# Two load queues for the chunk halves and a double-buffered conversion of w_out pieces in a one-core retention + MoE kernel

## The chip, the core and the metric

The kernel runs on one core of a Trainium2 chip. The metric is the device time of one execution in microseconds (us); the number compared is the median of several runs. Engine names are those of the profile: PE is TensorE (PEld its weight loads), DVE is VectorE, ACT is ScalarE, POOL is GpSimd, SP is SyncE, which here only issues DMAs. "SPq" and "ACTq" are the instruction queues of SP and ACT.

## What is computed

The reference chains three parts:

```
scores = q k^T / 8, times gamma_h^(i-j) for j <= i, else 0        (8 batches, 8 heads, 576 x 64)
x      = (scores v) gathered to 4608 tokens x 512
x      = gelu_sigmoid(x w_in) w_out                                (512 -> 2048 -> 512)
logits = x phi                                                     (4608 x 32)
d      = softmax of logits over the 4608 tokens;  slots = d^T x    (32 slots x 512)
slot results = relu(slots w1[e]) w2[e]                             (8 experts, 4 slots each)
out    = softmax of logits over the 32 slots, times slot results   (4608 x 512)
```

w_in and w_out come as 64-bit floating point numbers and are turned to 32-bit on the chip.

## The kernel before, in words

**Attention part.** The tokens are cut into 72 chunks of 64. For a chunk `g`, `scores(g)` (L182) multiplies queries and keys on PE, GpSimd scales the keys (L191) and VectorE masks the scores (L193, L194). `chunk_out(g)` (L196) makes the chunk's output on PE (L201, L202; it needs the masked scores), VectorE scales it into `xs` (L208, two buffers), ScalarE rounds it (L209) and GpSimd makes the remainder (L210). `state(g)` (L212) carries the running state. Each chunk's data lie in one of four `pack` buffers, which `load_chunk` (L173) fills with two half loads of 256 KB each, one for partitions 0 to 63 (L175) and one for partitions 64 to 127 (L176), both issued by SP. Parts of the packs that no load writes are cleared once by VectorE (L163, L164).

**Main part.** 384 tokens (6 chunks) make a block; there are 12. For each of 16 feature slices `fc`, `main_fc` (L331) does 12 matmuls into a `hp` buffer (three of them exist, L335 and L339) and ScalarE applies the gelu (L341). `turn_fc` (L343) turns the result: VectorE transposes it (L362), and after slices 7 and 15 SP issues 16 DMAs in a row that move it to the buffer `nat` (L368). `logits_group`, `softmax_part` and `slots_part` follow for the same or the block before. The chunks of block n+1 are worked in block n, at the slices in `CHUNK_AT`.

**Weights.** `load_raw` (L262) brings w_in (kind I) and a transposed w_out (kind O) in 32 loads of 512 KB into staging places: six early ones, then four rows of `ring` and `raw_tile` (L256). `convert` (L275) turns 64-bit numbers to 32-bit with one ScalarE (L279) and two VectorE instructions (L280, L281). The list `START` (L49) writes out the order of all this for block 0: T a chunk load, C constants, P phi, L the next raw load, A the next chunk step, I and O a conversion, M a slice of block 0.

**Pieces of w_out.** The slots need w_out once more in its natural layout. In blocks 1 to 8, four pieces per block (32 in all) are loaded (L318, 256 KB, at `fc % 4 == 0`), converted and stored to DRAM (L323, 128 KB, at `fc % 4 == 2`). All use the single buffer `raw`: load, conversion and store share it, so the load of a piece can start only when the store before it has landed.

**Expert weights.** `prefetch` (L449) brings 72 loads of 512 KB into places that come free late in the kernel: one `raw`, `NW2` = 9 in `pw2` after the attention buffers are closed, and others; the last blocks and the tail consume them.

**Who sets the order.** The source gives a program order. A planner (L745) then fixes, at build time and by its own estimate of times, one order for each engine and queue; it may take an instruction ahead of its place when its inputs and buffers are free in that estimate. On the chip each engine and queue goes strictly through its own list: what waits holds up everything behind it.

Of the kernel before, what the change touches and what calls it, by code (L numbers as in the profile page):

```python
# [9 lines left out]
F32 = mybir.dt.float32  # L10
F32R = mybir.dt.float32r
I32 = mybir.dt.int32
# [14 lines left out]
C = 64  # L27
NPB = S // C
NP = H // 2
# [4 lines left out]
NFC = DFF // 128  # L34
# [1 line left out]
NTILE = NT // 128  # L36
GF = 4
HF = NFC // 2
NW2 = 9
NW3, NW4 = 6, 5  # L40
DH = DM // 2

# [1 line left out]
PC = NP * C  # L44
# [2 lines left out]


START = (  # L49
    "T0 C T1 L L T2 L P A L A L L I L A L I L A L A I L A A I L M O L I L M O L I L A M O L I L M O I A M O I M A O I "  # L50
    "L M O I L A M I L O L L L L M A O I L M O I L M A O I L M I L O L L L M O M O M O M O"
).split()

ORDER = "IIIIOIOIOIOIOIOIOIIOOIOIOIIOOOOO"
EARLY = 18

# [56 lines left out]
def tile_kernel(ctx, tc, qkv, w_in, wo_t, w_out, phi, w1, w2, consts, out):  # L115
    nc = tc.nc
    pe, act, dve, pool, sp = nc.tensor, nc.scalar, nc.vector, nc.gpsimd, nc.sync
# [5 lines left out]
    px = ctx.enter_context(tc.tile_pool(name="px", bufs=1, reuse_waits="tile"))  # L123
# [4 lines left out]
    pa = att_ctx.enter_context(tc.tile_pool(name="pa", bufs=2, side="right", reuse_waits="tile"))  # L128

    ring = px.tile([128, 4, 2, 512], F32, name="ring")  # L130
# [27 lines left out]
    Q1, V0, KTB, KN, KTA, Q0, V1 = range(7)  # L158
    early_raw = pm.tile([128, 6, 1024], F32, tag="nat", name="early_raw")
    packs = []  # L160
    for i in range(NPACK):
        t = pa.tile([128, 7, NP, C], F32, name=f"pack{i}", bufs=1)
        dve.memset(t[0:C, 0:KN], 0.0)  # L163
        dve.memset(t[C:128, KTA:7], 0.0)  # L164
        packs.append(t)
    kts = []
    for i in range(2):
        t = pa.tile([128, 2, NP, D], F32, name=f"kt{i}", bufs=1)
# [4 lines left out]
    def load_chunk(g):  # L173
        t = packs[g % NPACK].rearrange("p c a d -> p (c a d)")
        sp.dma_start(t[0:C, KN * PC:7 * PC], qkv[g, 0:C])  # L175
        sp.dma_start(t[C:128, 0:KTA * PC], qkv[g, C:128])  # L176

    how = {"sub": {}}
    St = {}
# [16 lines left out]
    def chunk_out(g):  # L196
        n, off = divmod(g * C, NB)
        t = packs[g % NPACK]
        Op = ps.tile([128, NP, C], F32, tag="r", name="Op", bufs=3)
        for p in range(NP):  # L200
            pe.matmul(Op[0:C, p, :], t[:, V0, p], t[:, Q0, p], start=True, stop=True)  # L201
            pe.matmul(Op[C:128, p, :], t[:, V1, p], t[:, Q1, p], start=True, stop=True)  # L202
        if n not in xh:
            x = (pg if n % 2 == LAST % 2 else pb).tile([128, 2, NDC, NB], F32R, tag="x", name="x", bufs=1)
            xh[n], xl[n] = x[:, 0], x[:, 1]
        cols_ = slice(off, off + C)
        xs = pa.tile([128, NP, C], F32, tag="xs", name="xs")
        dve.tensor_tensor(xs, Op, osc, op=ALU.mult)  # L208
        act.copy(xh[n][:, :, cols_], xs)  # L209
        pool.tensor_tensor(xl[n][:, :, cols_], xs, xh[n][:, :, cols_], op=ALU.subtract)  # L210
# [31 lines left out]
    def chunk_items(n):  # L242

        if n >= NBLK:
            return []
        chunk_at = CHUNK_AT_LAST if n == LAST else CHUNK_AT
        return [(chunk_at[i], lambda g=g: chunk(g)) for i, g in enumerate(range(n * NB // C, (n + 1) * NB // C))]
# [4 lines left out]

    wo_dram = pd.tile([NFC // 2, 128, 2, DM], F32, name="wo_dram")
    wt, raws = {}, {}
    raw_tile = px.tile([128, 1024], F32, tag="raw", name="raw", bufs=1)
    late = [ring[:, i].rearrange("p a f -> p (a f)") for i in range(4)] + [raw_tile]  # L256

    free = {True: [early_raw[:, i] for i in range(6)], False: late}
    order = list(ORDER)
    loaded = {"I": 0, "O": 0}  # L260

    def load_raw():  # L262
        kind = order.pop(0)
        i = loaded[kind]
        loaded[kind] += 1
        early = sum(loaded.values()) <= EARLY and len(free[True]) > 0
        t = free[early].pop(0)
        raws[kind, i] = t, early
        (act if kind == "I" and i < 3 else sp).dma_start(
            t.bitcast(I32), (w_in if kind == "I" else wo_t)[i].bitcast(I32))  # L270

    def give_back(place):
# [2 lines left out]
    def convert(raw, out):  # L275
        two = raw.bitcast(I32).rearrange("p (f w) -> p f w", w=2)
        upper, lower = two[:, :, 1], two[:, :, 0]
        out = lower if out is None else out
        act.activation(upper.bitcast(F32), upper.bitcast(F32), AF.Prelu, scale=2.0 ** -112, alpha=2.0 ** 32)  # L279
        dve.tensor_scalar(lower, lower, 29, None, op0=ALU.logical_shift_right)  # L280
        dve.scalar_tensor_tensor(out, upper, 3, lower, op0=ALU.logical_shift_left, op1=ALU.bitwise_or)  # L281
        return upper.bitcast(F32), out.bitcast(F32)
# [28 lines left out]
            give_back(raws.pop(("O", 4 * g + a)))  # L311


    raw_n = {}

    def load_natural(i):
        raw_n[i] = px.tile([128, 1024], F32, tag="raw", name="raw", bufs=1)
        sp.dma_start(raw_n[i][:, 0:512].bitcast(I32), w_out[i // 2].bitcast(I32)[:, i % 2 * 512:i % 2 * 512 + 512])  # L318

    def convert_natural(i):  # L320
        t = raw_n.pop(i)
        _, w = convert(t[:, 0:512], t[:, 512:768].bitcast(I32))
        sp.dma_start(wo_dram[i // 4, :, i // 2 % 2, i % 2 * 256:i % 2 * 256 + 256], w)  # L323


    ring_pre = ring.rearrange("p a b f -> p (a b f)")[:, 0:4 * NB * 2].rearrange(
# [44 lines left out]
    def logits_group(n, g):  # L371
        if g == 0:
            Lg[n] = ps.tile([128, NB], F32, tag="L", name="Lg")
        for fl in range(GF):
            pe.matmul(Lg[n][32 * fl:32 * fl + 32, :], Wp[:, g * GF + fl, :], gT[n, g][:, fl, :],  # L375
                      start=(g == 0), stop=(g == NFC // GF - 1))
# [69 lines left out]
    def place_in(pool_, tag, bufs):  # L446
        return lambda: pool_.tile([128, 1024], F32, tag=tag, name="wx", bufs=bufs)

    def prefetch(place=None):  # L449
        if not todo:  # L450
            return
        key = todo.pop(0)
        if place is None:
            place = places.pop(0)
        t = place()
        places.append(place)
        if key[0] == 0:
            src = wo_dram[key[1]]
        elif key[0] == 1:
            src = w1[key[1], key[2] * 128:(key[2] + 1) * 128, :].rearrange("(c p) d -> p c d", p=128)  # L460
        else:
            _, c, e, i = key
            src = w2[c, e, i]
        t = t.rearrange("p (c d) -> p c d", c=src.shape[1])
        sp.dma_start(t, src)
        wx[key] = t

    def prefetch_views(t):
        for i in range(t.shape[1]):
            prefetch(lambda i=i: t[:, i])  # L470
# [40 lines left out]
    for n in range(1, NBLK):  # L511
        items = chunk_items(n + 1)
        ni, done = len(items), 0
        for fc in range(NFC):
            main_fc(n, fc)
            if n < LAST:
                turn_fc(n, fc)
            if fc % 4 == LOGITS_AT and fc >= 4:
                logits_group(n, (fc - 4) // 4)
            if fc == SOFTMAX_AT:  # L520
                logits_group(n - 1, 3)
                softmax_part(n - 1)
                if n == LAST:
                    combine_part(0, NTILE - NT128)
            if fc == SLOTS_AT:
                slots_part(n - 1)
            if 1 <= n <= NFC // 2:
                i = 4 * (n - 1) + fc // 4
                if fc % 4 == 0:
                    load_natural(i)  # L530
                elif fc % 4 == 2:
                    convert_natural(i)
            while done < ni and items[done][0] <= fc:
                items[done][1]()
                done += 1
            if n == LAST - 1:
                if fc == 9:
                    prefetch_views(pb.tile([128, 3, 1024], F32, tag="pre", name="wx", bufs=1))
                if done == ni and pw2 is None:
                    att_ctx.close()  # L540
                    prefetch(place_in(px, "raw", 1))
                    pw2 = ctx.enter_context(tc.tile_pool(name="pw2", bufs=NW2, side="right", reuse_waits="tile"))
                    for _ in range(NW2):
                        prefetch(place_in(pw2, "w", NW2))
            if n == LAST:
                if fc == 0:
                    prefetch_views(pb.tile([128, 3, 1024], F32, tag="x", name="wx", bufs=1))
                prefetch(place_in(pw, "w", NFC))
                if fc == 4:
                    prefetch_views(ring.rearrange("p a b f -> p a (b f)"))  # L550
                for i in range(5 if fc == 4 else fc > 4):
                    turn_fc(n, fc - (4 - i if fc == 4 else 0))
# [197 lines left out]
```

## Time and profile before

| | us |
|---|---|
| runs shown | 814.96, 816.33, 812.89 (median 814.96) |
| the profiled execution's own time | 817.49 |
| its span in the profile | 815.5 |
| PE busy in the span | 734.8 (90%) |
| DVE, ACT, POOL busy | 394.0, 241.2, 165.7 |

"Busy" is the time in which an engine had an instruction in work. The 12 blocks, the start (block 0 with the weight conversion) and the tail (experts and output) have different limits, so they are read one by one. PEclk is the granted clock of TensorE as a share of full speed (1.00 is 2.4 GHz, 0.50 is 1.2 GHz).

### The profile page before, as it was taken

What the parts mean: (1) busy time and instruction counts of PE and PEld (TensorE: products, weight loads), DVE (VectorE), ACT (ScalarE), POOL (GpSimd) and SP (SyncE); (2) the same over time, 40 slices, a digit from 0 to 9 for tenths busy, and PEclk for the clock granted to TensorE, in tenths of its full rate; (3) what the DMA queues carried; (4) which work ended last, traced back from release to release, by engine and by line L of the source; (5) the groups of instructions that cost most, each with busy time, mean ns of one, the idle gap of its engine ahead of it and who ended that gap; (6) DMA issues with size and microseconds to landing.
All of it is one profiled execution on the core that took longest, in us unless ns stands there. A gap on an engine that the chain in (4) does not pass through costs nothing.

```text
span 815.5 us, 17707 instructions
## 1 busy us (share of the span) xinstructions
PE 734.8 (90%) x7056; PEld 594.1 (73%) x7056; DVE 394.0 (48%) x1172; ACT 241.2 (30%) x491; POOL 165.7 (20%) x241
## 2 busy tenths in 40 slices
PE   3479979989989999799899799999999999996994
PEld 2468858768778697686787688887888878782453
DVE  5966373545356446536435555464455542313223
ACT  2433342323123213113123223231232312431323
POOL 4663230112121122111211212222112110000000
PEclk9679989999989999999999999999999999998997
DMA  9993772376476566565565666654547538898988
GB/s 247 330 228 100 192 236 74 108 164 160 121 165 156 124 149 151 123 155 137 123 159 127 150 151 145 152 130 95 136 108 157 130 64 315 270 374 315 409 345 334
DMA packets 76977, 148.98 MB, mean 183 GB/s; under 512 B 11232, under 2 KB 47840, under 8 KB 76896
## 3 DMA queue, kind: packets, MB, share of 16 engines
q1 hardware_dynamic: 76464, 146.29, 64.2%
q10 hardware_dynamic: 432, 1.57, 0.6%
q8 instruction: 55, 0.90, 0.5%
q14 instruction: 26, 0.21, 0.1%
HBM read 101.16 MB, written 13.63 MB: 141 GB/s over the span
## 4 chain that ended last, share of the span: by engine, by line
PE 49%; DMA 26%; SPq 12%; DVE 6%; issue 3%; ACT 2%; POOL 0%; ACTq 0%; DVEq 0%
PE hp L339 28%; DMA wo_dram<-raw 12%; SPq L368 9%; DMA raw<-in_moe_w_out_dram 9%; DMA early_raw<-in_moe_w_in_dram 4%; PE Lg L375 3%; PE Sg L423 2%; PE Op L201 2%; PE so_ps L670 2%; PE h_ps L606 2%; PE Sp L188 2%; SPq L176 1%; SPq L175 1%; PE St L227 1%; ACT raw L279 1%
## 5 line engine op out<-in xcount | busy, mean ns | idle before, releaser
L339 PE MATMUL hp<-x,w 128*128 128x384 f32 x2304 | 448.0, 348 | 9.7 <-ACT gT L341 5.8
L339 PEld LDWEIGHTS hp<-x,w 128*128 128x128 f32 x2304 | 404.1, 192 | 42.2 <-issue 18.4
L341 ACT ACTIVATE gT<-hp 128x384 f32<-128x384 f32 x192 | 91.1, 488 | 173.2 <-PE hp L339 170.5
L191 POOL TENSOR_TENSOR kt<-pack,cs 64x256 f32<-64x256 f32 x128 | 80.4, 628 | 254.8 <-PE St L228 78.1
L210 POOL TENSOR_TENSOR x<-xs,x 128x256 fp32r<-128x256 f32 x72 | 55.7, 773 | 224.2 <-ACT x L209 206.0
L362 DVE STREAM_TRANSPOSE ring<-gT 128x128 f32<-128x128 f32 x240 | 54.4, 280 | 79.6 <-ACT gT L341 79.4
L201 PEld LDWEIGHTS Op<-pack 128*64 128x64 f32 x576 | 43.4, 145 | 53.1 <-DVE pack L193 33.0
L201 PE MATMUL Op<-pack 128*64 128x64 f32 x576 | 56.0, 238 | 27.4 <-DVE pack L193 27.4
L362 DVE STREAM_TRANSPOSE pre<-gT 128x128 f32<-128x128 f32 x264 | 59.0, 278 | 44.8 <-ACT gT L341 44.8
L280 DVE TENSOR_SCALAR raw<-raw 128x256 int32<-128x256 int32 (+1 forms) x36 | 11.8, 327 | 124.8 <-DMA raw<-in_moe_w_out_dram 114.5
L187 PE MATMUL Sp<-pack 128*64 128x64 f32 x576 | 52.5, 238 | 14.7 <-DMA pack<-in_qkv_dram 14.7
L279 ACT ACTIVATE raw<-raw 128x256 f32<-128x256 f32 (+1 forms) x36 | 16.9, 471 | 161.8 <-DMA raw<-in_moe_w_out_dram 153.0
L209 ACT CAST x<-xs 128x256 fp32r<-128x256 f32 x72 | 29.1, 405 | 102.4 <-DVE xs L208 102.4
L187 PEld LDWEIGHTS Sp<-pack 128*64 128x64 f32 x576 | 44.8, 152 | 15.8 <-DVE early_raw L281 9.6
L227 PE MATMUL St<-pack,kt 128*64 128x64 f32 x512 | 48.7, 238 | 5.5 <-POOL kt L191 2.2
L188 PE MATMUL Sp<-pack 128*64 128x64 f32 x576 | 52.3, 240 | 1.0 <-DMA pack<-in_qkv_dram 1.0
L202 PE MATMUL Op<-pack 128*64 128x64 f32 x576 | 51.8, 237 | 1.0
L228 PE MATMUL St<-pack,kt 128*64 128x64 f32 x512 | 47.3, 239 | 0.2 <-POOL kt L191 0.2
L227 PEld LDWEIGHTS St<-pack,kt 128*64 128x64 f32 x512 | 39.6, 149 | 10.6 <-issue 5.2
L188 PEld LDWEIGHTS Sp<-pack 128*64 128x64 f32 x576 | 44.1, 150 | 3.6 <-issue 2.3
L202 PEld LDWEIGHTS Op<-pack 128*64 128x64 f32 x576 | 41.8, 145 | 3.3 <-DVE pack L194 2.5
L375 PE MATMUL Lg<-gT,Wp 128*32 128x384 f32 x384 | 44.2, 498 | 0.0
(124 smaller groups left out, 680.0 us busy)
## 6 DMA issues: line engine op xcount, KB each, us to landing
pack<-in_qkv_dram SPq DMA_DIRECT2D x144, 256.0 KB, 4.9
wx<-in_moe_w_dram SPq DMA_DIRECT2D x56, 512.0 KB, 9.5
nat<-pre SPq DMA_DIRECT2D x176, 96.0 KB, 2.2
nat<-ring SPq DMA_DIRECT2D x160, 96.0 KB, 2.2
out_dram<-ob SPq DMA_DIRECT2D x18, 512.0 KB, 3.3
raw<-in_moe_w_out_dram SPq DMA_DIRECT2D x32, 256.0 KB, 2.7
ring<-in_moe_wo_t_dram SPq DMA_DIRECT2D x10, 512.0 KB, 6.4
ring<-in_moe_w_dram SPq DMA_DIRECT2D x8, 512.0 KB, 10.2
```

The lines of the kernel that those rows point to most:

```text
L187: pe.matmul(Sp[C:128, p, :], t[:, KTA, p], t[:, Q0, p], start=True, stop=True)
L188: pe.matmul(Sp[0:C, p, :], t[:, KTB, p], t[:, Q1, p], start=True, stop=True)
L191: pool.tensor_tensor(kts[g % 2][r0:r0 + C, h], t[r0:r0 + C, KN], ksc[r0:r0 + C, cb, :].unsqueeze(2).to_broadcast([C, NP, D]), op=ALU.mult)
L201: pe.matmul(Op[0:C, p, :], t[:, V0, p], t[:, Q0, p], start=True, stop=True)
L202: pe.matmul(Op[C:128, p, :], t[:, V1, p], t[:, Q1, p], start=True, stop=True)
L210: pool.tensor_tensor(xl[n][:, :, cols_], xs, xh[n][:, :, cols_], op=ALU.subtract)
L227: pe.matmul(s_[0:C, p, :], kk[:, 0, p], t[:, V0, p], start=first, stop=True, skip_group_check=True)
L339: pe.matmul(hp, wt[fc][:, a, dc, :], b[n][:, dc, :], start=(i == 0), stop=(i == 3 * NDC - 1))
L341: act.activation(gT[n, g][:, fl, :], hp, AF.Gelu_apprx_sigmoid)
L362: dve.transpose(dst[:, c], src[:, c])
L368: sp.dma_start(nat[n][32 * b:32 * b + 32, :, a, hf * HF:(hf + 1) * HF, :], pre[n, hf][32 * a:32 * a + 32, b])
L375: pe.matmul(Lg[n][32 * fl:32 * fl + 32, :], Wp[:, g * GF + fl, :], gT[n, g][:, fl, :], start=(g == 0), stop=(g == NFC // GF - 1))
```

## The change

Each chunk's upper half load moves from SP's queue to ScalarE's. Two of the four packs are cleared by GpSimd instead of VectorE. `raw_tile` is no longer a staging place of the start; it is split in two halves of 512 columns, piece i of w_out uses half i % 2, and the loads run two pieces ahead. A converted piece goes to a separate tile `out_n` (one buffer); it is stored two slices after its conversion. `xs` has one buffer and `NW2` is 8. The first raw loads are split between ACT (w_in 0 and 2) and SP, where ACT issued w_in 0 to 2 before, and the lists `START`, `ORDER` and the number `EARLY` are rewritten.

```diff
-NW2 = 9
+NW2 = 8
 START = (
-    "T0 C T1 L L T2 L P A L A L L I L A L I L A L A I L A A I L M O L I L M O L I L A M O I L M O I A M O I M A O I "
-    "L M O I L A M I L O L L L L M A O I L M O I L M A O I L M I L O L L L M O M O M O M O"
+    "T0 C T1 L T2 L P A L L A L L I L A L A L I L A A I L A I L M O L I L M O L I L A M O I L M O L L I L A M O I M A "
+    "O I L M O I A O L L M I L M A O I L M O I L M A O I L M I L O L L L L M O M O M O M O"
-ORDER = "IIIIOIOIOIOIOIOIOIIOOIOIOIIOOOOO"
-EARLY = 18
+ORDER = "IIIIOIOIOIOIOIOIOIOIOIOIOIIOOOOO"
+EARLY = 19
...
-        dve.memset(t[0:C, 0:KN], 0.0)
-        dve.memset(t[C:128, KTA:7], 0.0)
+        own = dve if i < 2 else pool
+        own.memset(t[0:C, 0:KN], 0.0)
+        own.memset(t[C:128, KTA:7], 0.0)
...
         sp.dma_start(t[0:C, KN * PC:7 * PC], qkv[g, 0:C])
-        sp.dma_start(t[C:128, 0:KTA * PC], qkv[g, C:128])
+        act.dma_start(t[C:128, 0:KTA * PC], qkv[g, C:128])
...
-        xs = pa.tile([128, NP, C], F32, tag="xs", name="xs")
+        xs = pa.tile([128, NP, C], F32, tag="xs", name="xs", bufs=1)
...
-    raw_tile = px.tile([128, 1024], F32, tag="raw", name="raw", bufs=1)
-    late = [ring[:, i].rearrange("p a f -> p (a f)") for i in range(4)] + [raw_tile]
+    late = [ring[:, i].rearrange("p a f -> p (a f)") for i in range(4)]
...
-        (act if kind == "I" and i < 3 else sp).dma_start(
+        (act if i % 2 == 0 and kind == "I" and i < 4 else sp).dma_start(
...
-    raw_n = {}
+    raw_n, out_n = {}, {}
+    raw_tile = px.tile([128, 1024], F32, name="raw_tile")
 
     def load_natural(i):
-        raw_n[i] = px.tile([128, 1024], F32, tag="raw", name="raw", bufs=1)
-        sp.dma_start(raw_n[i][:, 0:512].bitcast(I32), w_out[i // 2].bitcast(I32)[:, i % 2 * 512:i % 2 * 512 + 512])
+        if i < 2 * NFC:
+            raw_n[i] = raw_tile[:, i % 2 * 512:i % 2 * 512 + 512]
+            sp.dma_start(raw_n[i].bitcast(I32), w_out[i // 2].bitcast(I32)[:, i % 2 * 512:i % 2 * 512 + 512])
 
     def convert_natural(i):
-        t = raw_n.pop(i)
-        _, w = convert(t[:, 0:512], t[:, 512:768].bitcast(I32))
-        sp.dma_start(wo_dram[i // 4, :, i // 2 % 2, i % 2 * 256:i % 2 * 256 + 256], w)
+        out_n[i] = px.tile([128, 256], F32, tag="out_n", name="out_n", bufs=1)
+        convert(raw_n.pop(i), out_n[i].bitcast(I32))
+
+    def store_natural(i):
+        sp.dma_start(wo_dram[i // 4, :, i // 2 % 2, i % 2 * 256:i % 2 * 256 + 256], out_n.pop(i))
...
                 i = 4 * (n - 1) + fc // 4
+                if i == 0 and fc == 0:
+                    load_natural(0)
+                    load_natural(1)
                 if fc % 4 == 0:
-                    load_natural(i)
+                    convert_natural(i)
                 elif fc % 4 == 2:
-                    convert_natural(i)
+                    store_natural(i)
+                    load_natural(i + 2)
...
-                    prefetch(place_in(px, "raw", 1))
+                    prefetch(lambda: raw_tile)
```

## Rows read from the trace of the kernel before

**Rows 1.** The profile page: busy time of each engine in the span, with its share, then the granted TensorE clock in 40 slices of the span (tenths of full speed).

```profile
PE 734.8 (90%) x7056; PEld 594.1 (73%) x7056; DVE 394.0 (48%) x1172; ACT 241.2 (30%) x491; POOL 165.7 (20%) x241
...
PEclk9679989999989999999999999999999999998997
```

**Rows 2.** Busy time by stage (the view of windows). Columns: the stretch, its length, busy us (and instructions) of PE, PEld, DVE, ACT and POOL, the granted clock, the DMA engines' busy share, GB/s. The stages are the start, the blocks in which pieces of w_out are worked, the blocks without them, the tail.

```profile
0.00:135.00 135.00, 99.35 (x972) 81.55 (x972) 83.72 (x172) 50.86 (x92) 55.77 (x68) 0.87 0.73 203
135.00:490.00 355.00, 329.71 (x3238) 276.83 (x3235) 177.96 (x592) 94.57 (x206) 68.16 (x109) 0.97 0.58 143
490.00:730.00 240.00, 240.00 (x2246) 202.21 (x2245) 107.72 (x347) 70.72 (x137) 38.97 (x62) 1.00 0.63 172
730.00:815.50 85.50, 65.77 (x608) 33.51 (x606) 24.60 (x64) 25.04 (x59) 2.83 (x3) 0.91 0.88 345
```

**Rows 3.** The same view, cut where slots_part's matmuls (L423) begin, once in each block: a first stretch with pieces up to the second such place, then five blocks with pieces, then three blocks without.

```profile
135.20:207.80 72.60, 68.23 (x644) 56.73 (x645) 38.05 (x127) 22.68 (x47) 13.76 (x22) 0.98 0.59 148
207.80:499.40 291.60, 270.68 (x2662) 228.57 (x2664) 146.03 (x484) 75.82 (x165) 56.91 (x90) 0.96 0.59 143
499.40:654.50 155.10, 155.10 (x1596) 131.44 (x1595) 77.91 (x262) 42.67 (x85) 32.80 (x53) 1.00 0.55 127
```

**Rows 4.** Who waited for whom from 135 to 490 us, for PE, DVE, ACT and SP's queue: us in total, times, the longest.

```profile
PE Op L201 <- DVE pack L193: 18.6, 10, 4.4
PE hp L339 <- ACT gT L341: 3.9, 2, 3.3
...
DVE raw L280 <- DMA raw<-in_moe_w_out_dram: 114.5, 31, 6.2
...
ACT raw L279 <- DMA raw<-in_moe_w_out_dram: 153.0, 32, 7.4
...
SPq L318 <- DMA wo_dram<-raw: 74.1, 31, 5.6
...
SPq L176 <- PE St L228: 1.2, 2, 0.8
...
SPq L175 <- PE hp L339: 0.6, 1, 0.6
```

**Rows 5.** The timeline around the longest stall of PE, in turn PE, DVE and SP's queue: start us, length us, engine, line, operation, count, and in brackets the idle time before it and what ended it.

```profile
454.27 0.33 PE L201 MATMUL Op<-pack 128*64 128x64 f32 x2 [4.38 <-DVE pack L193]
...
451.89 0.29 DVE L280 TENSOR_SCALAR raw<-raw 128x256 int32<-128x256 int32 x1 [4.00 <-DMA raw<-in_moe_w_out_dram]
...
453.79 0.43 DVE L193 TENSOR_TENSOR pack<-Sp,cs 64x256 f32<-64x256 f32 x1
...
447.27 0.33 SPq L323 DMA_DIRECT2D wo_dram<-raw  x1
449.21 0.33 SPq L318 DMA_DIRECT2D raw<-in_moe_w_out_dram  x1
```

**Rows 6.** The timeline of a stall that comes by way of ACT, ACT first, then PE.

```profile
167.99 0.44 ACT L279 ACTIVATE raw<-raw 128x256 f32<-128x256 f32 x1 [4.39 <-DMA raw<-in_moe_w_out_dram]
168.33 1.24 ACT L341 ACTIVATE gT<-hp 128x384 f32<-128x384 f32 x3
...
168.86 5.47 PE L339 MATMUL hp<-x,w 128*128 128x384 f32 x22 [3.29 <-ACT gT L341]
```

**Rows 7.** DMA issues of the page: KB each and the median us from issue to landing.

```profile
wo_dram<-raw SPq DMA_DIRECT2D x32, 128.0 KB, 2.8
```

**Rows 8.** SP's queue at the end of the start: a load whose place in the program is in the last block.

```profile
135.64 0.37 SPq L465 DMA_DIRECT2D ring<-in_moe_w_dram  x1
```

**Rows 9.** The view of windows in the start, columns as in rows 2.

```profile
20.00:30.00 10.00, 6.00 (x96) 5.38 (x96) 9.68 (x18) 4.86 (x9) 6.93 (x8) 0.93 1.02 404
...
40.00:50.00 10.00, 6.33 (x96) 5.70 (x96) 7.16 (x17) 2.80 (x5) 5.66 (x8) 0.55 1.03 251
50.00:60.00 10.00, 8.79 (x70) 5.94 (x71) 7.72 (x13) 4.28 (x8) 7.66 (x7) 0.83 0.94 212
```

**Rows 10.** DMA issues from 0 to 60 us: count, KB each, median us to landing.

```profile
pack<-in_qkv_dram SPq DMA_DIRECT2D x22, 256.0 KB, 10.6
```

**Rows 11.** The timeline of the first 13 us: ACT's queue, VectorE, GpSimd, and PE's first matmul.

```profile
0.73 1.38 ACTq L269 DMA_DIRECT2D early_raw<-in_moe_w_in_dram  x3
...
7.25 0.70 DVE L164 MEMSET pack<- 64x768 f32 x1 [0.20 <-issue]
...
10.87 0.43 DVE L280 TENSOR_SCALAR early_raw<-early_raw 128x512 int32<-128x512 int32 x1 [1.40 <-DMA early_raw<-in_moe_w_in_dram]
...
1.76 0.31 POOL L171 MEMSET kt<- 64x256 f32 x1
12.32 1.34 POOL L191 TENSOR_TENSOR kt<-pack,cs 64x256 f32<-64x256 f32 x2 [10.25 <-DMA cs<-in_consts_dram]
...
9.62 0.45 PE L187 MATMUL Sp<-pack 128*64 128x64 f32 x2 [9.62 <-DMA pack<-in_qkv_dram]
```

**Rows 12.** Waits of SP's queue in the first 20 us.

```profile
SPq L175 <- DMA early_raw<-in_moe_w_in_dram: 1.4, 1, 1.4
```

**Rows 13.** One line's instructions over the whole span: the last reader of `xs` on GpSimd, then one of the 16 DMA issues in a row; count, ns min/median/max, first and last start us.

```profile
L210 POOL TENSOR_TENSOR x<-xs,x x72: 722/734/1324, 20.3 to 679.8; 128x256 fp32r<-128x256 f32 x72
...
L368 SPq DMA_DIRECT2D nat<-pre x176: 588/605/1756, 85.3 to 673.0; - x176
```

**Rows 14.** PE's waits from 600 us to the end, longest first.

```profile
PE dp L410 <- DVE dT L405: 2.3, 1, 2.3
```

More of the change, by code (lines that the diff above doesn't have):

```diff
@@ L49 @@
 START = (
-    "T0 C T1 L L T2 L P A L A L L I L A L I L A L A I L A A I L M O L I L M O L I L A M O L I L M O I A M O I M A O I "
-    "L M O I L A M I L O L L L L M A O I L M O I L M A O I L M I L O L L L M O M O M O M O"
+    "T0 C T1 L T2 L P A L L A L L I L A L A L I L A A I L A I L M O L I L M O L I L A M O I L M O L L I L A M O I M A "
+    "O I L M O I A O L L M I L M A O I L M O I L M A O I L M I L O L L L L M O M O M O M O"
 ).split()
-ORDER = "IIIIOIOIOIOIOIOIOIIOOIOIOIIOOOOO"
-EARLY = 18
+ORDER = "IIIIOIOIOIOIOIOIOIOIOIOIOIIOOOOO"
+EARLY = 19
 CHUNK_AT = (0, 2, 5, 8, 10, 12)
```

## The prediction

> **What bounds the kernel now.** I read the page's busy line first: PE is in work 90% of the span (its weight loads, beside it, 73%) and no other engine above half [rows 1], so time can only be gained where PE stands still or runs slowly. The stages say where that is [rows 2]. From 490 to 730 us PE is busy all of the time at clock 1.00: nothing to gain there. From 135 to 490 it is idle 355.0 - 329.7 = 25.3 us, in the start 135 - 99.4 = 35.7 us, in the tail 19.7 us.
>
> The middle stage differs from the full one only by the 32 pieces of w_out, so I price them by comparing blocks [rows 3]. Three blocks without pieces take 155.1 / 3 = 51.7 us each. Five blocks with pieces take 291.6 us against 5 x 51.7 = 258.5: 33.1 us too much. Of these, 291.6 - 270.7 = 20.9 are idle PE; the other 12.2 are PE working at the lower clock, since the granted clock, which drops from 2.4 to 1.2 GHz for a while after stalls, has a mean of 0.96 (0.04 x 291.6 = 11.7). The stretch before adds 72.6 - 68.2 = 4.4 us idle and 0.02 x 72.6 = 1.5 of clock. So the pieces cost 33.1 + 5.9 = **39 us** today, and that is the ceiling of what their rearrangement can give.
>
> The table of waits names the chain [rows 4]. SP waits 31 times, 74.1 us in all, to issue a piece's load (L318) until the store of the piece before has landed; VectorE then waits 31 times, 114.5 us, at L280 for that load, ScalarE 153.0 us at L279. PE's own waits are for masked scores (L193) and gelus (L341), which neither read a piece. The timeline shows the link [rows 5]: the store goes out at 447.27, the load behind it at 449.21, VectorE stands at L280 until 451.89, and L193, queued behind, runs at 453.79, so that PE was idle 4.38 us. The second link is ScalarE: it stands 4.39 us at L279, three gelus are queued behind, and PE is idle 3.29 us [rows 6].
>
> **The change part by part.**
>
> *Pieces, double-buffered.* The load of piece i+2 needs only that piece i has been converted, so the store leaves the loop of load and conversion, and a load has a whole piece's time to land. The waits of L279 and L280 for loads should go, and with them the 39 us. What is late next: L281 now writes `out_n`, of which there is one, so it must wait for the store before it to land; behind it on VectorE stand L193 and the transposes L362, on which PE and the `nat` transfers wait. In program order the store has two slices, 51.7 / 16 x 2 = 6.5 us, against 2.8 us to landing [rows 7]: no wait. But the planner pulls things ahead: the 32 pieces, whose program place reaches to block 8, are done before 499 us, in block 7 [rows 3], and a load of the last block was issued at 135.64 [rows 8]. Pulled together, every piece could wait as SP does now, 74.1 / 31 = 2.4 us, against VectorE's 114.5 / 31 = 3.7 [rows 4]. Then 2.4 / 3.7 = 65% of the cost stays. The gain is thus between 0.35 x 39 = 14 us and 39. I take the middle, **-27 us**.
>
> *Half loads on two queues, steady blocks.* ScalarE issues 6 more DMAs per block at 1.38 / 3 = 0.46 us [rows 11], 2.8 us of a block in which it is busy 42.7 / 3 = 14.2 of 51.7 [rows 3]. Hidden by its idle time: 0. If ScalarE has to wait before it may issue, gelus are held up: see the third rival.
>
> *Half loads, start.* From 20 to 60 us the DMA engines are busy all along, yet the rate is 404 GB/s in a stretch of 128-partition weight loads and 251 where the 64-partition halves are mixed in [rows 9]. The 22 halves up to 60 us [rows 10] are 5.77 MB: 23.0 us at 251 GB/s and 14.3 at 404, so -8.7 us if two queues make the two halves run side by side. The other end is the lowest rate there, 212: 27.2 us, +4.2. Nothing before has the halves on two queues; the nearest row is the 251, where both halves are already in flight together behind each other. I take that: 0.
> The Trainium skill speaks against the change here: the page SBUF — State Buffer, section "Can I just issue two DMAs to hit both halves?", says that two transfers to the two partition halves run on the same engines one after the other, about 6% faster than one alone. By that page the sum would hold -1.3 us here, by the rows' upper rate -8.7; no row of before shows which.
>
> *Clears, list, staging.* Four of VectorE's eight clears leave, 4 x (0.70 + 0.20) = 3.6 us in its first 8 us, but at 10.87 it waits for a weight load anyway [rows 11]: 0. GpSimd gets them: a 64x768 clear is three times the 64x256 one of 0.31 us, so 3.7 us in all, and its first other work is at 12.32: 0. The new list puts the first chunk's halves ahead of the weights; PE's first matmul waited for them until 9.62 [rows 11], and 4 us of that may go. Against it, `raw_tile` is no staging place any more, and since it is then free from the first microsecond, pieces can be pulled into the start, each 384 KB or 1.0 us at 404 GB/s, where the DMA engines are full [rows 9]. Four such pieces eat the 4 us. Start in sum: 0, bounds -13 (4 + 8.7) and +12 (4.2 for the rate and eight pieces).
>
> *`xs` with one buffer.* It is free again when GpSimd's L210, 0.73 us [rows 13], is through; chunks come every 51.7 / 6 = 8.6 us. That spacing covers it: 0.
>
> *One place fewer for expert weights.* One 512 KB load moves into the tail, 524 KB / 345 GB/s = 1.5 us [rows 2]. PE's waits from 600 us on are led by the softmax (2.3 us), and no weight load is among them [rows 14]: 0, bound +1.5.
>
> **Sum.** 817.5 (the profiled execution) - 27 = 790.5. That execution stands 2.5 us above the median of the runs, so the forecast for the median is **788 us**. What a measurement of this kernel can tell from no change is about 0.5%, or 4 us.
>
> **The rivals.**
>
> *The wait moves to `out_n`.* Conversions pulled together wait for the store each time. For it: the pieces do run ahead of their place, and one output buffer is all there is. Against it: only one transfer is left in the loop. Gain 14: 815 - 14 = 801. Chance 0.15.
>
> *The start pays.* Pieces pulled ahead, and 32 raw loads through ten staging places instead of eleven, lengthen a start that is full of DMA and where VectorE is busy 9.68 of 10 us [rows 9]. Ten pieces are +10 us: 815 - 27 + 10 = 798. Chance 0.13.
>
> *ScalarE held up by its DMA queue: slower.* SP's queue has waited at a chunk load for a weight load that ScalarE had issued and that has nothing to do with the chunk [rows 12], so an issue may wait for an earlier transfer of the other queue. Such a wait on ScalarE stops the gelus. The place is the row of 16 issues at L368, 0.6 us each [rows 13], which leaves SP some 10 us behind. One case like rows 6 costs 3.3 us of idle PE and, as the 12.2 + 1.5 us of clock spread over PE's 12 waits of rows 4, 1.1 us at the lower clock: 4.4. From 27 / 4.4 = 6 cases on, the gain is gone; one in each of ten blocks gives 815 - 27 + 44 = 832. Against it: from 135 to 490 us SP waited next to nothing at chunk loads (0.6 and 1.2 us [rows 4]). Chance 0.12.
>
> *The two halves do overlap.* -8.7 us more: 779. Chance 0.10. It would be the one part that does what the rates in rows 9 allow and the page named above denies.
>
> **How the numbers follow.** The forecast, stage cleared by most and the start about even, has 0.50; its own range is 772 (39 gained, start -4) to 806 (14 gained, start +5). Faster by over 0.5%: 0.49 of it, 0.12 of the first rival, 0.09 of the second (a little more start and it is gone), all 0.10 of the fourth: 0.80. Within 0.5%: 0.01 + 0.03 + 0.02 + 0.01 = 0.07. Slower: 0.02 of the second and 0.11 of the third: 0.13. The range 769 to 814 leaves out the third rival and the far ends, where several bounds fall together, of the others.
>
> **What would show it.** Right: L279 and L280 no longer head the waits for loads; PE idle under 10 us and clock 0.99 or 1.00 between the first and eighth block; SP's wait at L318 gone. First rival: VectorE at L281 waiting for `wo_dram`. Second: loads of pieces in the first 60 us and a later end of the start. Third: PE waiting for gelus, ScalarE standing before its DMA issues, also in blocks that were full before. Fourth: over 300 GB/s where halves are loaded, and the first chunks sooner. I am wrong if blocks with pieces still take over 56 us each, or if the blocks without grow beyond 52.

## The result and the profile after

The changed kernel takes 794.39 us (median of 4 runs, 792.32 to 795.43); the kernel before 814.65 beside it. The ratio is 0.9748, 95% interval 0.9719 to 0.9778: 2.5% faster. The forecast was 788 us, range 769 to 814. The profiled execution took 795.43 us, span 793.5.

In the changed kernel `main_fc`'s matmuls are L343, the gelu L345, VectorE's transposes L366, a piece's load L320, its conversion L279 to L281, its store L327, a chunk's two half loads L176 and L177. The page's busy line and clock, to be laid beside [rows 1]:

```profile
PE 724.6 (91%) x7056; PEld 584.8 (74%) x7056; DVE 397.1 (50%) x1168; ACT 244.7 (31%) x491; POOL 167.9 (21%) x245
...
PEclk9769998989999999999999999999999999998998
```

That hides what happened. The windows view shows it when it is cut as in [rows 3], where `slots_part`'s matmuls begin: to block 0's, block 1's, block 6's, block 9's and block 11's. The kernel after:

```profile
0.00:171.00 171.00, 124.42 (x1169) 103.79 (x1169) 111.36 (x252) 66.06 (x129) 61.70 (x76) 0.88 0.82 228
171.00:217.10 46.10, 45.37 (x445) 35.15 (x445) 27.20 (x89) 16.04 (x32) 11.04 (x18) 0.96 0.76 182
217.10:474.40 257.30, 257.30 (x2658) 218.23 (x2657) 133.25 (x440) 70.96 (x142) 55.88 (x90) 1.00 0.57 128
474.40:629.60 155.20, 155.20 (x1599) 131.57 (x1599) 77.26 (x262) 42.61 (x85) 32.78 (x53) 1.00 0.55 123
629.60:714.70 85.10, 81.27 (x616) 64.95 (x618) 26.68 (x74) 27.47 (x51) 3.96 (x7) 1.00 0.76 256
714.70:793.50 78.80, 61.09 (x580) 31.13 (x580) 21.35 (x55) 21.61 (x52) 2.50 (x3) 0.91 0.89 352
```

The kernel before, the stretches that [rows 3] does not have:

```profile
0.00:158.20 158.20, 121.91 (x1156) 101.71 (x1157) 96.43 (x215) 59.98 (x109) 58.44 (x72) 0.89 0.69 193
158.20:207.80 49.60, 45.87 (x465) 36.68 (x465) 25.54 (x84) 13.76 (x29) 11.09 (x18) 0.97 0.65 153
654.50:739.70 85.20, 81.39 (x612) 65.04 (x611) 26.63 (x74) 27.50 (x51) 3.92 (x7) 0.99 0.79 271
739.70:815.50 75.80, 59.88 (x580) 30.66 (x580) 21.45 (x55) 21.46 (x52) 2.57 (x3) 0.91 0.87 347
```

Stretch by stretch: the start **+12.8** (158.2 to 171.0), the next block -3.5, the five blocks after it **-34.3** (291.6 to 257.3, PE without a gap and at clock 1.00), the three blocks that were full before +0.1, the last two -0.1, the tail +3.0: together -22.0. The start did not stay even. One line says why: the 32 loads of pieces, which the program has in blocks 1 to 8, were issued from 25.9 to 216.5 us (columns: count, ns min/median/max, first and last start us).

```profile
L320 SPq DMA_DIRECT2D raw_tile<-in_moe_w_out_dram x32: 327/383/946, 25.9 to 216.5; - x32
```

So the five blocks from 217.1 us on are full with nearly all their pieces done before; what the pieces still cost stands in the start, where VectorE is busy 111.4 us instead of 96.4 and the DMA engines 82% of 171 us instead of 69% of 158.

The third rival is seen there too. The view of the timeline, ACT's issue of a half load and what is behind it, then GpSimd, then PE:

```profile
33.26 0.47 ACTq L177 DMA_DIRECT2D pack<-in_qkv_dram  x1
33.77 0.65 ACT L279 ACTIVATE early_raw<-early_raw 128x512 f32<-128x512 f32 x1 [6.32 <-DMA ring<-in_moe_wo_t_dram]
34.33 0.39 ACT L210 CAST x<-xs 128x256 fp32r<-128x256 f32 x1
...
34.80 0.94 POOL L211 TENSOR_TENSOR x<-xs,x 128x256 fp32r<-128x256 f32 x1 [6.42 <-ACT x L210]
...
36.48 0.48 PE L228 MATMUL St<-pack,kt 128*64 128x64 f32 x2 [3.83 <-POOL kt L192]
```

ScalarE does nothing for 6.3 us and goes on when a transfer of weights on SP's queue, which the chunk does not use, has landed; its chunk rounding is behind that, GpSimd waits for the rounding, PE for GpSimd 3.83 us. Why the two are tied stands in the trace's instruction records: the DMAs of this program take turns on eight completion semaphores, counters that a transfer raises when it has landed, and an issue first waits for the transfer that had its semaphore before. The half load issued at 33.26 and the weight load issued at 20.45 both have number 107; that load landed at 33.10. The wait of [rows 12] is of the same kind: SP's half load at 4.96 us shares number 100 with the weight load of ScalarE that landed at 4.95. So the hold comes from the program as it was built; no run shows the two queues holding each other up without it.

### The profile page after: what moved, and what is told of

Its sections match the earlier page's. It is cut to its first block, busy times and chain, and to the rows that moved or that the text cites. A ratio compares the mean times of both kernels' runs of the same rounds, so it can differ in the third digit from the quotient of the medians.

```text
span 793.5 us, 17765 instructions
## 1 busy us (share of the span) xinstructions
PE 724.6 (91%) x7056; PEld 584.8 (74%) x7056; DVE 397.1 (50%) x1168; ACT 244.7 (31%) x491; POOL 167.9 (21%) x245
## 3 DMA queue, kind: packets, MB, share of 16 engines
q1 hardware_dynamic: 70848, 127.94, 57.4%
## 4 chain that ended last, share of the span: by engine, by line
PE 81%; DMA 10%; DVE 4%; ACT 1%; issue 1%; POOL 1%; SPq 0%; DVEq 0%; ACTq 0%; POOLq 0%
PE hp L343 49%; PE Lg L379 5%; PE Sg L427 5%; PE Op L202 4%; PE Sp L189 3%; DMA ring<-in_moe_wo_t_dram 3%; PE St L228 3%; DMA pack<-in_qkv_dram 2%; PE h_ps L614 2%; PE so_ps L678 2%; DMA raw_tile<-in_moe_w_out_dram 2%; DMA wo_dram<-out_n 2%; DMA cs<-in_consts_dram 1%; PE op L696 1%; PE St L229 1%
## 5 line engine op out<-in xcount | busy, mean ns | idle before, releaser
L343 PE MATMUL hp<-x,w 128*128 128x384 f32 x2304 | 441.5, 346 | 7.1 <-ACT w L289 5.3
L343 PEld LDWEIGHTS hp<-x,w 128*128 128x128 f32 x2304 | 399.2, 190 | 39.2 <-issue 14.7
L345 ACT ACTIVATE gT<-hp 128x384 f32<-128x384 f32 x192 | 92.3, 490 | 238.5 <-PE hp L343 238.3
L366 DVE STREAM_TRANSPOSE ring<-gT 128x128 f32<-128x128 f32 x240 | 55.7, 283 | 115.8 <-ACT gT L345 115.7
L366 DVE STREAM_TRANSPOSE pre<-gT 128x128 f32<-128x128 f32 x264 | 60.1, 281 | 69.8 <-ACT gT L345 69.8
L211 POOL TENSOR_TENSOR x<-xs,x 128x256 fp32r<-128x256 f32 x72 | 54.0, 750 | 162.5 <-ACT x L210 162.0
L188 PE MATMUL Sp<-pack 128*64 128x64 f32 x576 | 49.5, 233 | 12.6 <-DMA pack<-in_qkv_dram 8.4
L228 PE MATMUL St<-pack,kt 128*64 128x64 f32 x512 | 47.9, 234 | 14.4 <-POOL kt L192 10.6
L228 PEld LDWEIGHTS St<-pack,kt 128*64 128x64 f32 x512 | 38.7, 146 | 20.2 <-POOL kt L192 15.7
L188 PEld LDWEIGHTS Sp<-pack 128*64 128x64 f32 x576 | 42.8, 148 | 13.3 <-issue 9.0
L189 PE MATMUL Sp<-pack 128*64 128x64 f32 x576 | 49.6, 234 | 0.0
L229 PE MATMUL St<-pack,kt 128*64 128x64 f32 x512 | 45.4, 234 | 0.7 <-POOL kt L192 0.5
L189 PEld LDWEIGHTS Sp<-pack 128*64 128x64 f32 x576 | 42.4, 146 | 0.2 <-issue 0.2
L229 PEld LDWEIGHTS St<-pack,kt 128*64 128x64 f32 x512 | 37.6, 146 | 4.7 <-issue 3.4
L427 PE MATMUL Sg<-nat,dn 128*32 128x512 f32 x288 | 37.5, 644 | 1.8 <-DVE dn L416 1.8
```

The source lines that it names most:

```text
L188: pe.matmul(Sp[C:128, p, :], t[:, KTA, p], t[:, Q0, p], start=True, stop=True)
L189: pe.matmul(Sp[0:C, p, :], t[:, KTB, p], t[:, Q1, p], start=True, stop=True)
L228: pe.matmul(s_[0:C, p, :], kk[:, 0, p], t[:, V0, p], start=first, stop=True, skip_group_check=True)
L229: pe.matmul(s_[C:128, p, :], kk[:, 1, p], t[:, V1, p], start=first, stop=True, skip_group_check=True)
L343: pe.matmul(hp, wt[fc][:, a, dc, :], b[n][:, dc, :], start=(i == 0), stop=(i == 3 * NDC - 1))
L345: act.activation(gT[n, g][:, fl, :], hp, AF.Gelu_apprx_sigmoid)
```

## The experiments

Each ratio is against the kernel before on the same chip. The table puts the profiles side by side by the time at which block 0's, 1's, 6's and 11's `slots_part` begins on PE, and the end.

| kernel | ratio (95%) | block 0 | block 1 | block 6 | block 11 | span |
|---|---|---|---|---|---|---|
| before | | 158.2 | 207.8 | 499.4 | 739.7 | 815.5 |
| after | 0.9748 (0.9719 to 0.9778) | 171.0 | 217.1 | 474.4 | 714.7 | 793.5 |
| e1_pieces_only | 0.9871 (0.9828 to 0.9914) | 160.8 | 213.6 | 487.4 | 727.8 | 804.3 |
| e2_two_queues_only | 0.9880 (0.9824 to 0.9937) | 162.6 | 211.8 | 491.3 | 731.5 | 809.4 |
| e3_held | 0.9706 (0.9659 to 0.9752) | 155.5 | 206.8 | 475.4 | 715.6 | 792.7 |
| e4_one_queue | 0.9739 (0.9688 to 0.9789) | 169.3 | 218.0 | 474.9 | 715.0 | 792.2 |
| e9_out_in_ring | 0.9706 (0.9657 to 0.9756) | 152.6 | 203.1 | 472.0 | 712.2 | 790.9 |
| e10_out_in_ring_nw9 | 0.9717 (0.9671 to 0.9763) | 151.4 | 202.3 | 470.6 | 710.9 | 788.1 |
| e11_anchored | 0.9554 (0.9508 to 0.9600) | 157.7 | 200.8 | 458.9 | 699.0 | 776.5 |
| e12_before_anchored | 0.9917 (0.9879 to 0.9954) | 153.6 | 204.6 | 488.3 | 734.5 | 810.5 |
| e13_anchored_one_queue | 0.9641 (0.9600 to 0.9681) | 153.9 | 201.7 | 465.8 | 708.6 | 784.9 |
| e14_zeros | 0.9986 (0.9952 to 1.0019) | 157.2 | 208.0 | 498.9 | 739.3 | 816.0 |

**One part alone.** e1 takes the new handling of the pieces, with `raw_tile` kept as a staging place of the start; e2 moves the upper half loads alone.

```diff
(e1, on the kernel before: the change's load_natural, convert_natural, store_natural, xs, NW2, and)
-    raw_tile = px.tile([128, 1024], F32, tag="raw", name="raw", bufs=1)
+    raw_tile = px.tile([128, 1024], F32, name="raw_tile")
     late = [ring[:, i].rearrange("p a f -> p (a f)") for i in range(4)] + [raw_tile]
(e2, on the kernel before)
-        sp.dma_start(t[C:128, 0:KTA * PC], qkv[g, C:128])
+        act.dma_start(t[C:128, 0:KTA * PC], qkv[g, C:128])
```

> The kernel before with the new handling of the pieces alone (two halves of raw_tile, loads two ahead, out_n, late store, xs with one buffer, NW2 = 8); raw_tile stays a staging place of the start, so no piece can be loaded before some 135 us; lists, clears and queues as before. Theory A (the gain is the load and store leaving VectorE's and ScalarE's path; the longer start comes from pieces pulled into it): slots_part of block 0 at about 158 us as before, blocks at 51 to 53 us each from the third on, tail +3: 778 to 785 us. Theory B (the blocks of the changed kernel are full only because the pieces were done elsewhere, in the start and block 1): stalls come back in the blocks, 803 us or more. Theory C (the gain is SP's queue relieved of half the chunk loads): 805 us or more.

> The kernel before with one line changed: the upper half loads are issued by ScalarE. Theory C: about 795 us. Theory A: the chain load, conversion, store is untouched, 815 us within 5. If the two halves run side by side on two queues, the first block's main matmuls start several us before 55 us and the DMA rate from 40 to 60 us rises from 231 to 300 GB/s or more; if not, they start at 55 within 2.

e1 refutes theory A: 808.84 us lies in the ranges of B and C. It gains 1.3%: its pieces come from 136 to 306 us, the blocks after are full (51.4, 52.7, 50.2 us), but the three before them take 52.8, 64.7 and 54.7, so stalls come back where pieces are worked, as B has it. e2 takes 810.83 us beside 817.55 for the kernel before on its chip, a gain of 1.2%, where C wanted 795 and A no change. Its start is 4.4 us longer, and its rate from 40 to 60 us is 204 GB/s, so the halves do not run side by side; but the five blocks take 279.5 us instead of 291.6, though no line of the pieces was touched. Two lines from 211.8 to 491.3 us in e2, and as the third PE's wait in the same five blocks of the kernel before (207.8 to 499.4 us):

```profile
211.80:491.30 279.50, 264.97 (x2661) 222.65 (x2661) 144.76 (x484) 76.28 (x165) 56.57 (x90) 0.99 0.63 149
...
PE Op L201 <- DVE pack L193: 12.1, 9, 2.1
...
PE Op L201 <- DVE pack L193: 18.6, 10, 4.4
```

PE stands less and the clock is 0.99 instead of 0.96 [rows 3]. That SP's queue, with 6 issues fewer in a block, was part of the chain is the likely reason, but e2's trace does not show it: a store follows its conversion after 3.9 us in the mean instead of 4.1, and loads land as fast as before (2.7 us). e11 against e13 below shows it better.

**Pieces held out of the start.** One edit on the changed kernel (e3), and the two queues taken back (e4).

```diff
(e3, on the changed kernel; raw_tile is defined ahead of it)
-    late = [ring[:, i].rearrange("p a f -> p (a f)") for i in range(4)]
+    late = [ring[:, i].rearrange("p a f -> p (a f)") for i in range(4)] + [raw_tile]
(e4, on the changed kernel)
-        act.dma_start(t[C:128, 0:KTA * PC], qkv[g, C:128])
+        sp.dma_start(t[C:128, 0:KTA * PC], qkv[g, C:128])
```

> The changed kernel with one edit: raw_tile is again the fifth late staging place of the start, so that the pieces are held until the start has given it back. Theory A: no piece before some 130 us, the start 9 to 13 us shorter, the blocks still full from the third on: 780 to 786 us. Theory D (the start is longer because of the new list or the two queues): still 792 to 797. Theory B: 803 or more.

> The changed kernel with both halves on SP's queue again. Theory C: most of the gain is lost, 808 us or more. Theory A: 794 us within 5. Theory D with the two queues as the cause: the start gets shorter, 785 or less.

e3 shows both halves of the story. Its first piece is loaded at 123 us and the start is 15.5 us shorter than the changed kernel's: the pieces had lengthened it. But the kernel is no faster, since the next block but one takes 61.9 us instead of 52.7. Theory A was wrong on the total; 794.72 us lies in D's range, but D's cause is ruled out by the shorter start. The waits of VectorE and PE in that block, from 206.8 to 268.7 us (in e3 and e9 the conversion is L280 to L282):

```profile
DVE out_n L282 <- DMA wo_dram<-out_n: 13.6, 6, 5.8
DVE raw_tile L281 <- DMA raw_tile<-in_moe_w_out_dram: 5.0, 6, 1.1
...
PE Op L202 <- DVE pack L194: 4.4, 3, 3.2
```

This is the first rival: the conversion stands for the store before it, and the masked scores stand behind. e4, 798.27 us, shows no difference from the changed kernel, as A had it and against C: there, where nearly all pieces are done before the five blocks (e4's last load is at 198 us), the two queues are worth nothing that the intervals can tell. The gains of e1 and e2 add up to that of the change, but e4 has all of it without the two queues, so the parts do not simply add. The new lists (`START`, `ORDER`, `EARLY`) were not run alone; what they are worth is not shown.

**More output places.** e9 gives conversions four places in `ring`'s idle fourth row; e10 also gives the kilobyte back to `xs` and `NW2`.

```diff
(e9, on e3)
-        out_n[i] = px.tile([128, 256], F32, tag="out_n", name="out_n", bufs=1)
+        out_n[i] = ring[:, 3].rearrange("p a f -> p (a f)")[:, i % 4 * 256:i % 4 * 256 + 256]
(e10, on e9)
-NW2 = 8
+NW2 = 9
...
-        xs = pa.tile([128, NP, C], F32, tag="xs", name="xs", bufs=1)
+        xs = pa.tile([128, NP, C], F32, tag="xs", name="xs")
```

> e3_held (pieces held until the start has given raw_tile back) with one edit: a converted piece goes to one of four places in the fourth row of ring, which is idle after the start, instead of the single out_n. Theory A2 (the stall left in blocks 1 to 3 of e3_held is VectorE at the conversion waiting for the store before, rival one of the prediction): the block that took 61.9 us takes 54 or less, no wait of the conversion for the store: 782 to 788 us. Theory B2 (the pieces load the blocks by their work and traffic, not by the wait for the store): 792 to 797 as e3_held.

> e9_out_in_ring with the kilobyte that out_n took given back: xs has two buffers and NW2 = 9 again. Theory E (the 3 us that the changed kernel is longer after its last block come from the one place fewer for expert weights): the stretch from the last slots_part to the end 75.8 us instead of 78.8, 3 us below e9. Rival (they come from the transfers' order in the tail): 78 to 79 us, same as e9.

The wait for the store is gone, and the block takes 64.5 us all the same: VectorE now stands for the load. Waits in that block of e9, 203.1 to 267.6 us:

```profile
DVE raw_tile L281 <- DMA raw_tile<-in_moe_w_out_dram: 20.9, 10, 5.0
...
PE Op L202 <- DVE pack L194: 6.4, 3, 3.5
```

Theory A2 is wrong: the planner pulls the pieces still closer (32 loads from 122 to 261 us), and the load, which was no wait to speak of in e3, becomes one. The time, 793.55 us, is in B2's range; e11 decides against B2's cause. e10 is no faster than e9; its tail is 77.2 us, e9's 78.7, between theory E and its rival.

**The pieces spaced by force.** A copy of one column makes each load depend on the slice at which the program has it.

```diff
(e11, on the changed kernel; called where load_natural(0), (1) and (i + 2) were)
+    def anchored_load(i, n, fc):
+        if i < 2 * NFC:
+            dve.tensor_copy(raw_tile[:, i % 2 * 512:i % 2 * 512 + 1], gT[n, fc // GF][:, fc % GF, 0:1])
+        load_natural(i)
(e12, on the kernel before, in load_natural ahead of the load)
+        dve.tensor_copy(raw_n[i][:, 0:1], gT[n, fc // GF][:, fc % GF, 0:1])
```

> The changed kernel with one addition: before each load of a piece VectorE copies one column of the gelu result of the slice at which the program has that load into the load's half of raw_tile, so that the load can't be issued before that slice is done; the planner can't pull the pieces ahead any more. Theory F (what is left of the pieces' cost, some 15 us in the start of the changed kernel or in blocks 1 to 3 of e3_held and e9, comes from pieces pulled close together, so that whatever the chip does slower than planned becomes a wait): pieces some 13 us apart up to block 8, slots_part of block 0 at 155 to 158 us, every block 50 to 53: 783 us, at most 787. Theory G (they cost the blocks by their work and traffic): the cost spreads over blocks 1 to 8, 792 us or more.

> The kernel before with the same addition: one buffer for the pieces as before, but each load held to its slice. Theory F2 (spacing alone does it, the double buffer is not needed): start as before, blocks 50 to 53 us: 786 to 790 us. Theory A3 (with one buffer the load is still too late for its conversion two slices on, and VectorE stands as before): 805 us or more.

> e11_anchored with both half loads on SP's queue. If the two queues are worth nothing (as m1 and m2 have it for the rate, 238 against 245 GB/s): within 4 us of e11. If issuing the halves at the same time does help the blocks or the start: 5 us or more above e11.

e11 is what theory F says, and the fastest kernel here: 779.63 us, 4.5% under the kernel before. Its loads run from 133.4 to 512.9 us. The same cuts as above, from the start to block 9:

```profile
0.00:157.70 157.70, 120.06 (x1170) 100.72 (x1170) 95.68 (x215) 58.20 (x108) 60.77 (x76) 0.90 0.73 194
157.70:200.80 43.10, 42.88 (x448) 34.50 (x444) 24.88 (x85) 14.69 (x30) 11.09 (x18) 1.00 0.79 173
200.80:458.90 258.10, 257.92 (x2662) 218.81 (x2661) 142.78 (x493) 78.73 (x161) 56.41 (x90) 1.00 0.67 154
458.90:613.80 154.90, 154.90 (x1597) 132.00 (x1600) 82.46 (x283) 44.69 (x90) 32.92 (x53) 1.00 0.63 140
```

Theory G is refuted with it. The start is as short as before, and blocks that work pieces take 258.1 us for five, as those of the changed kernel that work none. Yet VectorE still waits; its waits and PE's longest from 157.7 to 613.8 us:

```profile
DVE raw_tile L280 <- DMA raw_tile<-in_moe_w_out_dram: 57.4, 24, 4.3
...
DVE out_n L281 <- DMA wo_dram<-out_n: 8.4, 7, 2.1
...
PE lt L394 <- DVE Lp L391: 0.2, 1, 0.2
```

57.4 us of waits cost PE next to nothing, presumably because with pieces 13 us apart nothing urgent is queued behind them. e12, 812.45 us, gains 0.8% only, in A3's range, and is no clean test of spacing without the double buffer: its copy writes the one buffer, so VectorE itself stands for the store, 55.9 us, which the kernel before never did, and PE then waits for the softmax. e13 takes 787.64 us, ratio 0.9641: with spaced pieces the two queues are worth about 8 us. On one queue the start is 3.8 us shorter, but a piece's load leaves SP's queue later (after its copy, 75.2 us for the 32 pieces in sum against 54.6 in e11) while it lands no slower (104.4 us in sum against 109.2). So it is the place in SP's queue that tells there, and not how fast a piece lands. VectorE's waits for pieces rise. From 153.9 to 623.4 us in e13:

```profile
DVE raw_tile L280 <- DMA raw_tile<-in_moe_w_out_dram: 81.3, 28, 4.2
...
DVE out_n L281 <- DMA wo_dram<-out_n: 30.8, 10, 3.7
```

**The loads by themselves.** m1 and m2 leave only the 72 chunk loads and 18 stores of zeros of the kernel before, the loads on one queue and on two.

```diff
(m2, on m1)
-        sp.dma_start(t[C:128, 0:KTA * PC], qkv[g, C:128])
+        act.dma_start(t[C:128, 0:KTA * PC], qkv[g, C:128])
```

> Of the kernel before only the 72 chunk loads into the four packs are left, both halves on SP's queue, and then 18 stores of zeros to the output; no attention, no weights, no experts. 37.7 MB at the 250 GB/s of the mixed stretches of the start would be 150 us, at 404 GB/s 93 us.

> The same with the upper halves on ScalarE's queue. If two queues let the halves run side by side: 350 GB/s or more, a third less time for the loads than m1. If two transfers to the two partition halves run one after the other whoever issues them, as the page SBUF — State Buffer of the Trainium skill has it: within 6% of m1.

m1 took 189.7 us, m2 179.4, one run each: 5% less. The stores, over all 128 partitions, run from 52 to 101 us in m1 and from 29 to 74 us in m2. In stretches of loads alone, m1's windows, the last two columns being DMA share and GB/s:

```profile
10.00:29.00 19.00, 0.00 (x0) 0.00 (x0) 1.00 1.05 226
110.00:150.00 40.00, 0.00 (x0) 0.00 (x0) 1.00 1.05 240
```

and m2's:

```profile
10.00:29.00 19.00, 0.00 (x0) 0.00 (x0) 1.00 1.04 248
110.00:150.00 40.00, 0.00 (x0) 0.00 (x0) 1.00 1.04 244
```

Two queues add 2% to 10%, and neither stretch comes near the 404 GB/s of 128-partition loads [rows 9]. The Trainium skill's page SBUF — State Buffer, section "Can I just issue two DMAs to hit both halves?", has +6% for two transfers to the two halves over a single one. That is not quite this comparison, since m1 too has several halves on the way at a time, but it points the same way: the halves do not run side by side.

**What was priced at nothing.** Clears, `xs` and `NW2` together on the kernel before (e14).

```diff
-NW2 = 9
+NW2 = 8
...
-        dve.memset(t[0:C, 0:KN], 0.0)
-        dve.memset(t[C:128, KTA:7], 0.0)
+        own = dve if i < 2 else pool
+        own.memset(t[0:C, 0:KN], 0.0)
+        own.memset(t[C:128, KTA:7], 0.0)
...
-        xs = pa.tile([128, NP, C], F32, tag="xs", name="xs")
+        xs = pa.tile([128, NP, C], F32, tag="xs", name="xs", bufs=1)
```

> The kernel before with the three edits that the prediction priced at nothing, together: half of the clears on GpSimd, xs with one buffer, NW2 = 8. If each is covered as argued: 815 us within 4 against the kernel before on the same chip, ratio 0.995 to 1.005, the first main matmul at 55 us within 1, the stretch from the last slots_part to the end 76 to 79 us. If one place fewer for expert weights is what lengthens the tail: 3 us more after the last slots_part, and the ratio above 1.002.

Ratio 0.9986 (0.9952 to 1.0019), tail 76.7 us: nothing, as priced. The first main matmul came at 52.8 us, 1.2 sooner than the band allowed, without effect on block 0's end.

## Why the prediction came out right, point by point

- **Bottleneck and ceiling: right.** The stall ran from store to load to VectorE to masked scores. 39 us were set as the ceiling; the stretch from block 0's `slots_part` to block 6's went from 341.2 to 303.4 us, -37.8 (in e11 to 301.2, -40.0). The signs named for it came: PE is idle 0.7 us in that stretch, and VectorE's wait for pieces fell from 114.5 to 10.4 us, ScalarE's from 153.0 to 36.2.
- **Pieces, -27: the sum near, the reason only half.** "A load has a whole piece's time to land" is not what emptied the blocks. The pieces left them: nearly all were worked before block 2. Where they are kept in the blocks close together (e1, e3, e9), one block takes 62 to 65 us, with a single output place or with four. The first rival's wait is there in part: VectorE stands 17.6 us at L281 for stores in the changed kernel, 12.1 of it in the start. Against e11 the pulled pieces still cost e3 18.3 us from block 0 to block 3 and the changed kernel 13.3 in its start.
- **Start, 0: wrong, the mis-sized term.** It is +12.8 up to block 0's `slots_part`, just outside the stated bound of +12. The failed step was "four such pieces eat the 4 us": 23 of the 32 pieces were loaded by 160 us. Held out (e3, e11), the start is 155.5 and 157.7 us, so 13 to 15 us are the pieces' price there. This is the second rival, priced at +10 on top of the gain: its 798 us is nearer to the measured 794.39 than the forecast's 788.
- **Half loads on two queues: the rate right, the rest missed.** No rise of the rate to 404 (m1, m2), which ends the fourth rival. The third rival's hold is real in the start, though it comes from a shared semaphore; with two queues the start is 2 to 4 us longer (e4 against after, e13 against e11, e2 against before), and that the holds are all of this is not shown. In the full blocks PE waits for nothing of the kind. The gain I had not priced is that of the two queues where pieces are worked: 12 us in e2's five blocks, 8 us in all in e11, where the loads' later place in SP's queue shows.
- **Clears, `xs`, expert places: right**, nothing (e14). The tail's +3.0 us is not explained by `NW2`: with 8 places tails are 76.3 to 78.8 us (e1, e3, e4, e9, e11, e13, e14, after), with 9 they are 75.8 to 77.9 (before, e2, e10, e12). What moves it stays open.
- **Sum.** -22.0 in the profiled pair against -27: -37.8 in the blocks, +12.8 in the start, +3.0 in the tail. That the sum came within 5 us is partly luck: the blocks gave 11 us more and the start took 13 us more than priced, and the two errors nearly cancel.

## What to carry to other kernels

When a planner sets each engine's order, a freed buffer is also a permission to run early: look where the work goes, and give it a dependence on the step beside which it should run. Waits on an engine in strict order cost by what is queued behind them, not by their sum: 57.4 us cost next to nothing in e11, while 18.6 us of VectorE's waits in e3 stand in a block that is 10 us longer than a full one. Moving a load to another queue can be worth its place in the first queue though it adds little to the rate. And a wait between two queues can come from a completion semaphore that the build gave to both: look at its number before blaming the queues.

## What the runs showed of the hardware

Loads of the two partition halves alone, on one queue against two: 240 against 244 GB/s in a long stretch, 226 against 248 at the beginning, while a stretch of mostly 128-partition weight loads went at 404 [rows 9]. ScalarE did nothing for 6.3 us while an issue on its queue waited for a transfer of SP's queue to land; the wait is on the semaphore that both use.
